# Sixteen half-height transposes instead of eight full ones, in four units of a retention and SiLU kernel

## The chip, the cores and the metric

The kernel runs on one core of one Trainium2 chip. Its time is the device time of one execution in microseconds (us). TensorE (PE) multiplies matrices and writes to PSUM, a memory of eight banks of 128 partitions; VectorE (DVE) and ScalarE (ACT) do element-wise work and bring results from PSUM to SBUF; GpSimd (POOL) prepares data; SyncE (SP) issues most DMA transfers. Each engine works through its own list of instructions in order and waits on semaphores of the others.

## The reference

A retention recurrence over 768 positions, for 4 batches and 8 heads of 64, followed by a feed-forward block with a SiLU:

```
for t in range(S):                       # S = 768
    state = gamma * state + outer(k[:, :, t], v[:, :, t])
    y[:, :, t] = (1 / sqrt(D)) * q[:, :, t] @ state        # D = 64
x = y as (3072, 512)                     # 4 * 768 tokens, 8 heads * 64
h = x @ w_in                             # w_in 512 x 2048
out = (h * sigmoid(h)) @ w_out           # w_out 2048 x 512
```

`gamma` has one value for each head. Results are float32.

## The kernel before

The recurrence is computed in chunks of 128 positions. A **unit** is one chunk of one batch, so there are 6 x 4 = 24 units, numbered chunk by chunk: unit n is chunk n // 4 of batch n % 4. For each unit the kernel does the following:

- *Transposes* (`stage_t`, L441): k and q arrive as 128 positions (partitions) by 8 heads by 64. Four transposes each on TensorE, one per pair of heads, against a 128x128 identity, put them into one PSUM bank each, `kp` and `qp`; ScalarE copies each bank as a whole into SBUF, `kt` and `qt` (L450). These are 128 partitions (two heads by 64) by 4 pairs by 128 positions.
- *Scores and sums* (`stage_s` L464, `stage_a` L474): within a unit the 128 positions are two halves of 64. Products of k and q inside a half, and of k and v for the running state, are 64x64 matmuls on quarters of the array, into the bank pair `sc`. `stage_s` reads k after it was multiplied by decay factors (`scale_k`, L390), which is done in place once the transposes have read it. For units 10 to 13 ScalarE does it, one head at a time (L399), four heads directly and four from the list `behind_copy`.
- *Masking and state* on VectorE (`steps_a`: `am` L482, `mid` L490, `state` L494), and scaling of `qt` (`scale_q`, L411).
- *Output of the unit* (`stage_y`, L513): more 64x64 matmuls into the bank pair `y`, in two parts. A small POOL instruction (`fence`, L385) stands between them.
- *Splitting* (`split_x`, L569 to L575) into three parts, which are the input `xt` of the feed-forward block.

From unit 14 on (`FAR`) k and q are turned by DMA instead, and no transposes run on TensorE.

The feed-forward block works on groups (c, f), chunk c and 128 of the 2048 hidden columns. A group is 12 matmuls of 128x512 (`multiply`, L666) into two banks, `ha` and `hb`. ScalarE copies `ha` (L676), VectorE subtracts `hb` (L681), ScalarE applies the SiLU (L686), and SP stores the group (`gd<-g`, L692). The banks `ha`, `hb` and `kp` take turns on three PSUM banks (`turn`, L376); `qp` has a bank of its own. The results wait in three buffers with the tag `hs` until their stores have landed.

Weights arrive as 64-bit numbers and are converted on the way: one ScalarE instruction (`ca`, L202), six on VectorE (L205 to L223), and then a split into three parts on both engines (`wi`: L120, L123, L126, L128). A group cannot run before its slice is there.

TensorE's order is that of the program text. The other engines' lists are written out by hand up to the first group of chunk 1 (L894 to L899). After that a planner orders them, with `queue(instruction)` holding a piece of work behind a named instruction; `evac[0]`, the last copy of the transposes, is one of these. Units 10 to 13 come just behind that point: the visits of units 10, 11 and 12 lie in two halves between the groups listed in `pairs` (L905), and unit 13 follows the last of them in one piece.

Of the kernel before, what the change touches and what calls it, by code (L numbers as in the profile page):

```python
# [13 lines left out]
FP32 = mybir.dt.float32  # L14
# [19 lines left out]
def kernel(  # L34
# [28 lines left out]
    nc = tc.nc  # L63
    B, H, S, D = q.shape
    DM, DF = moe_w_in.shape
    C = 128
    NC = S // C
    HP = H // 2
# [12 lines left out]
    def pool(name, bufs, **kw):  # L81
        return ctx.enter_context(tc.tile_pool(name=name, bufs=bufs, **kw))
# [6 lines left out]
    one = pool("one", 1)  # L89
# [49 lines left out]
    kqv = {"k": {}, "q": {}, "v": {}}  # L139
    EARLY = 2 * B  # L140

    FAR = 3 * B + 2
    LATER = 4 * B + 2
    early = {}

    def load(name, n):
        if n >= len(units):
            return
        c, b = units[n]
        src = {"k": k, "q": q, "v": v}[name]  # L150
        if n == 4 * B and name == "k":
            t = conv.tile([128, H, D], FP32, tag="wl", name=f"kf_{n}")
            nc.sync.dma_start(out=t, in_=src[b, :, ds(c * C, C)].rearrange("h t d -> t h d"))
            kqv[name][n] = t
            return
        if n < EARLY:

            if n not in early:
                early[n] = wpool.tile([128, 3, H, D], FP32, tag=f"w{4 + n}", name=f"kqv_{n}")
            t = early[n][:, "kqv".index(name)]  # L160
        else:
            t = ld.tile([128, H, D], FP32, tag=f"{name}f", name=f"{name}f_{n}",
                        bufs=2 if name == "q" else 3)
        nc.sync.dma_start(out=t, in_=src[b, :, ds(c * C, C)].rearrange("h t d -> t h d"))
        kqv[name][n] = t
# [86 lines left out]
    evac, held, w_sb = [], [], {}  # L252
    written = [True]

    def queue(ins):

        return ExitStack() if written[0] or ins is None else tc.issue_after(ins)
# [58 lines left out]
    ident = const.tile([128, 128], FP32, tag="ident", name="ident")  # L316
# [45 lines left out]
    xt, kt, qt, am = {}, {}, {}, {}  # L362
# [8 lines left out]
    def banks(tag, name, n=2):  # L371
        return ps_u.tile([128, n, 512], FP32, tag=tag, name=name)
# [3 lines left out]
    def turn(name):  # L376
        turns[0] += 1
        return ps_h.tile([128, 512], FP32, tag=f"h{turns[0] % 3}", name=name)
# [11 lines left out]
    def scale_k(n):  # L390
        if 0 <= n < len(units):
            t = kqv["k"][n]
            if units[n][0] == NC - 1:
                t = t[:D]
            if 2 * B + 1 < n < 3 * B + 2:

                def half(heads):
                    for h in heads:
                        nc.scalar.activation(out=t[:, h, :], in_=t[:, h, :], func=AF.Copy,  # L399
                                             scale=gk[:, units[n][0], h : h + 1])  # L400

                half(range(H // 2))
                behind_copy.append(lambda: half(range(H // 2, H)))
                return
            g = gk[: t.shape[0], units[n][0], :].unsqueeze(2).to_broadcast([t.shape[0], H, D])
            nc.vector.tensor_tensor(out=t, in0=t, in1=g, op=ALU.mult)
# [33 lines left out]

    def stage_t(n):  # L441

        for name, to, bufs, src, tp in (
                ("kt", kt, 2, kqv["k"][n], turn(f"kp_{n}")),
                ("qt", qt, 3, kqv["q"].pop(n), banks("q", f"qp_{n}", 1)[:, 0])):
            tp = tp.rearrange("p (a t) -> p a t", a=HP)
            for a in range(HP):
                nc.tensor.transpose(tp[:, a, :], src[:, 2 * a : 2 * a + 2, :], ident)
            to[n] = one.tile([128, HP, C], FP32, tag=name, name=f"{name}_{n}", bufs=bufs)
            evac[:] = [nc.scalar.copy(out=to[n], in_=tp).ins]  # L450

    def score_tile(n):
        u = banks("s", f"sc_{n}")
# [156 lines left out]
    def halves(m):  # L610

        first, mid, last = (0 <= m - i < len(units) for i in range(3))
        if first and m < FAR:
            stage_t(m)
# [5 lines left out]
        if mid:  # L620
# [9 lines left out]
            if m > 3 * B + 1 and units[m - 1][1] == B - 1:  # L630

                behind_copy.append(next_chunk)
        if first and m < LATER - 1 and m != FAR:
            with queue(masked[0]) if m > FAR else ExitStack():
                scale_k(m)
# [3 lines left out]

        n = m if m >= LATER else m + 1  # L640
        if FAR < n < len(units) and (m < LATER - 1 or m >= LATER):
            with queue(fenced[0]):
                part_t(n)
        for name in "kqv":
            for n in (m + 1, m + 2):
                if (n, name) not in apart and EARLY <= n <= LATER and n == (
                        m + 1 if name == "v" or n >= LATER else m + 2):
                    load(name, n)
# [6 lines left out]

    apart = [(FAR + 1, "k"), (FAR + 1, "q"), (FAR + 2, "q")]
    pending, stored = [], []
# [88 lines left out]
    def T(n):  # L746
        stage_t(n)
# [185 lines left out]
    first_far = steps.index((2, 3))  # L933
    parts = {first_far: FAR}
    turns_at = {first_far + 2: FAR}
    turns_at.update({far[m] + 1: m + 1 for m in range(FAR, LATER - 1)})
    joins_at = {far[m] + 1: m for m in range(FAR, LATER)}
# [47 lines left out]
    for c in range(NC):  # L985
# [9 lines left out]
        for f in range(NF):  # L995
            n = c * NF + f
# [3 lines left out]
            t = ready[n]  # L1000
# [17 lines left out]
        for b in range(B):  # L1018
            oa, ob = acc[b]
            o = one.tile([128, DM], FP32, tag=("kt", "qt")[b % 2], name=f"o_{c}_{b}",  # L1020
                         bufs=(2, 3)[b % 2])
# [8 lines left out]
            n = 2 if b == B - 1 else 1  # L1030
# [36 lines left out]
```

## Time and profile before

| | us |
|---|---|
| median of 4 runs | 618.06 (617.33 to 620.19) |
| the profiled execution | 618.18 |
| its span | 616.2 |
| TensorE busy | 597.9 |
| VectorE busy | 425.2 |
| ScalarE busy | 315.8 |
| one transpose, k or q, as recorded (L448) | 0.27 |
| one copy of its bank (L450), kt and qt | 0.57 and 0.59 |

The granted TensorE clock was 0.999 over the span. The span runs from the first to the last instruction; the execution's time is 2.0 us longer. Engine names in the lines are PE, PEld (TensorE's weight loads), DVE, ACT, POOL and SP. `out<-in` names the tiles that an instruction writes and reads, without buffer numbers; `x4` counts instructions; a 64x64 float32 matmul has two records, a transpose has one. A bracket at the end of a line tells how long the engine sat idle before it, and what ended the wait. Matmuls overlap, so the recorded length of one is longer than the distance from its start to the start of the next.

The transposes of units 10 to 13 start at 57.27, 66.22, 75.17 and 84.13 us.

### The profile page before, as it was taken

Reading aid. Unit: us, or ns where it says so; the run is one execution under the profiler, and the core shown is the slowest. Engines: PE = TensorE matmul, PEld = TensorE weight load, DVE = VectorE, ACT = ScalarE, POOL = GpSimd, SP = SyncE. Lnnn points to the kernel's source line nnn. Section 1 sums busy time; section 2 is a strip of 40 time slices with the busy share of each in tenths; the row PEclk is TensorE's granted clock in tenths of the full one; section 3 lists DMA queues with packets and bytes.
Section 4 is the critical chain, followed back from the end, with each engine's and each line's share of the span. In section 5 each row is a group of like instructions: output and inputs, shape, how many; then the busy total and the mean of one; then the engine's idle time right before and its main releaser. Section 6 shows DMA issues by size and latency. Waiting matters only on the chain.

```text
span 616.2 us, 13460 instructions
## 1 busy us (share of the span) xinstructions
PE 597.9 (97%) x5360; PEld 491.7 (80%) x5360; DVE 425.2 (69%) x731; ACT 315.8 (51%) x595; POOL 29.5 (5%) x85
## 2 busy tenths in 40 slices
PE   5798999999999999999999999999999999999997
PEld 4677887888778888888788888888888888888886
DVE  4899989799988777786699774635545463644631
ACT  7678886676667567666588732312221321312311
POOL 3000000100031111220000000000000000000000
PEclk9999999999999999999999999999999999999999
DMA  9998865784789699999777542532423433432301
GB/s 193 224 234 213 236 193 171 196 245 162 261 216 211 188 270 246 275 231 313 256 250 246 197 129 68 173 101 103 170 71 136 137 105 101 148 125 94 112 1 68
DMA packets 144334, 108.88 MB, mean 177 GB/s; under 512 B 101136, under 2 KB 109584, under 8 KB 144272
## 3 DMA queue, kind: packets, MB, share of 16 engines
q1 hardware_dynamic: 141392, 102.79, 59.2%
q10 hardware_dynamic: 2880, 5.24, 2.3%
q8 instruction: 42, 0.69, 0.5%
q14 instruction: 20, 0.16, 0.1%
HBM read 66.06 MB, written 36.70 MB: 167 GB/s over the span
## 4 chain that ended last, share of the span: by engine, by line
PE 76%; DVE 5%; ACT 1%; issue 1%; DMA 1%; DVEq 0%; POOLq 0%
PE o L1007 21%; PE ha L666 20%; PE oa L1007 14%; PE hb L666 10%; PE ob L1007 7%; PE y L513 2%; DVE g L681 1%; DMA yr<-yd 1%; PE sc L474 1%; PE sc L464 1%; DVE ca L218 1%; DVE xt L572 1%; PE o L1015 0%; DVE xt L575 0%; DVE cw L223 0%
## 5 line engine op out<-in xcount | busy, mean ns | idle before, releaser
L666 PE MATMUL ha<-xt,wi 128*128 128x512 f32 x768 | 193.8, 394 | 1.4 <-ACT xt L569 0.7
L666 PEld LDWEIGHTS ha<-xt,wi 128*128 128x128 f32 x768 | 141.8, 188 | 33.7 <-ACT wi L126 1.2
L1007 PE MATMUL o<-wo,gs 128*128 128x512 f32 x564 | 143.2, 389 | 0.0
L733 DVE TENSOR_TENSOR gs<-gr,gs 128x512 fp32r<-128x512 f32 x96 | 62.2, 685 | 90.3 <-ACT gs L731 90.3
L1007 PEld LDWEIGHTS o<-wo,gs 128*128 128x128 f32 x564 | 105.9, 188 | 21.9
L731 ACT ACTIVATE gs<-gr 128x512 fp32r<-128x512 f32 x96 | 53.6, 621 | 134.2 <-issue 131.8
L1007 PE MATMUL oa<-wo,gs 128*128 128x512 f32 x376 | 115.8, 389 | 0.0
L666 PE MATMUL hb<-xt,wi 128*128 128x512 f32 x384 | 102.9, 390 | 0.3 <-DVE xt L575 0.2
L681 DVE TENSOR_TENSOR g<-g,hb 128x512 f32<-128x512 f32 x96 | 65.5, 683 | 34.7 <-ACT g L676 21.8
L666 PEld LDWEIGHTS hb<-xt,wi 128*128 128x128 f32 x384 | 71.9, 188 | 16.1 <-DVE xt L575 0.7
L686 ACT ACTIVATE g<-g 128x512 f32<-128x512 f32 x96 | 60.2, 628 | 45.4 <-DVE g L681 45.4
L1007 PEld LDWEIGHTS oa<-wo,gs 128*128 128x128 f32 x376 | 70.6, 188 | 14.7
L1007 PE MATMUL ob<-wo,gs 128*128 128x512 f32 x188 | 73.7, 392 | 0.0
L676 ACT ACTIVATE g<-ha 128x512 f32<-128x512 f32 x96 | 57.0, 593 | 27.9 <-PE ha L666 14.6
L734 DVE SCALAR_TENSOR_TENSOR gs<-gs 128x512 fp32r<-128x512 f32 x96 | 62.0, 683 | 0.0
L1007 PEld LDWEIGHTS ob<-wo,gs 128*128 128x128 f32 x188 | 35.3, 188 | 8.7 <-DVE o L1025 1.6
L202 ACT ACTIVATE ca<-wf 128x512 f32<-128x512 f32 x32 | 21.4, 668 | 7.3 <-DVE cw L223 5.0
L1024 ACT ACTIVATE o<-o 128x512 f32<-128x512 f32 x10 | 6.0, 600 | 33.4 <-PE o L1007 33.0
L218 DVE SCALAR_TENSOR_TENSOR ca<-wf,ca 128x512 f32<-128x512 uint32 x32 | 22.7, 710 | 0.5
L482 DVE TENSOR_TENSOR am<-sc,decay 128x512 f32<-128x512 f32 x24 | 16.5, 687 | 9.5 <-PE sc L474 9.4
L212 DVE SCALAR_TENSOR_TENSOR cs<-ca,cs 128x512 uint32<-128x512 uint32 x32 | 22.1, 690 | 0.9
L513 PE MATMUL y<-qt,mid 64*64 64x64 f32 x384 | 19.7, 220 | 1.8 <-POOL token L385 1.8
(93 smaller groups left out, 563.2 us busy)
## 6 DMA issues: line engine op xcount, KB each, us to landing
gd<-g SPq DMA_DIRECT2D x96, 256.0 KB, 3.5
gr<-gd SPq DMA_DIRECT2D x96, 256.0 KB, 2.7
wf<-in_moe_w_out_dram SPq DMA_DIRECT2D x16, 512.0 KB, 5.0
out_dram<-o ACTq DMA_DIRECT2D x20, 256.0 KB, 2.1
wf<-in_moe_w_in_dram SPq DMA_DIRECT2D x16, 256.0 KB, 4.2
wf<-in_moe_w_in_dram SPq DMA_DIRECT2D x32, 128.0 KB, 3.9
kf<-in_k_dram SPq DMA_DIRECT2D x16, 256.0 KB, 4.2
qf<-in_q_dram SPq DMA_DIRECT2D x16, 256.0 KB, 4.2
```

Source lines behind the costliest of these rows:

```text
L202: nc.scalar.activation(out=a.bitcast(FP32), in_=hi.bitcast(FP32), func=AF.Abs, scale=65536.0)
L212: nc.vector.scalar_tensor_tensor(out=s, in0=a, scalar=3, in1=s, op0=ALU.logical_shift_left, op1=ALU.bitwise_or)
L218: nc.vector.scalar_tensor_tensor(out=p.bitcast(FP32), in0=lo, scalar=2.0 ** -52, in1=p.bitcast(FP32), op0=ALU.mult, op1=ALU.mult)
L513: i = nc.tensor.matmul(yp[ts(e, D), o, a, :], lhsT=lhsT, rhs=rhs, start=(e, o) not in started, stop=True, skip_group_check=True).ins
L666: nc.tensor.matmul(hb if i == 2 else ha, lhsT=w_sb[f][:, i, ts(kk, 128)], rhs=xt[c][:, i, kk, :], start=kk == 0 and i != 1, stop=kk == KIN ...
L676: copied[:] = [nc.scalar.activation(out=hs, in_=ha, func=AF.Copy, scale=ONE_E).ins]
L681: taken_out[:] = [nc.vector.tensor_tensor(out=hs, in0=hs, in1=hb, op=ALU.subtract).ins]
L686: nc.scalar.activation(out=hs, in_=hs, func=AF.Silu)
L731: nc.scalar.activation(out=t[:, 0, :], in_=g, func=AF.Copy, scale=HALF)
L733: nc.vector.tensor_tensor(out=t[:, 1, :], in0=g, in1=high, op=ALU.subtract)
L734: nc.vector.scalar_tensor_tensor(out=t[:, 2, :], in0=t[:, 1, :].bitcast(FP32), scalar=-1.0 / EPS, in1=high, op0=ALU.mult, op1=ALU.add)
L1007: nc.tensor.matmul(o, lhsT=g, rhs=wo[f][:, i, :], start=f == 0 and i != 1, stop=f == NF - 1 and i != 0)
```

## The change

For units 10 to 13 (`ROWS`), each transpose of 128 positions becomes two of 64 positions: one reads partitions 0 to 63 with the upper left 64x64 of the identity, the other partitions 64 to 127 with the lower right. They alternate, so that neighbours use different halves of the array's rows. The bank `kp` now holds the first 64 positions of both k and q, the bank `qp` the last 64. Each bank is brought out by two copies of 128x256, one into half the positions of `kt`, one of `qt`; that makes four copies a unit instead of two. `evac` holds the last of the four. All other units stay as they were.

```diff
     FAR = 3 * B + 2
+    ROWS = range(2 * B + 2, FAR)
...
     def stage_t(n):
 
-        for name, to, bufs, src, tp in (
-                ("kt", kt, 2, kqv["k"][n], turn(f"kp_{n}")),
-                ("qt", qt, 3, kqv["q"].pop(n), banks("q", f"qp_{n}", 1)[:, 0])):
-            tp = tp.rearrange("p (a t) -> p a t", a=HP)
+        src = kqv["k"][n], kqv["q"].pop(n)
+        tp = turn(f"kp_{n}"), banks("q", f"qp_{n}", 1)[:, 0]
+
+        def new(name, to, bufs):
+            to[n] = one.tile([128, HP, C], FP32, tag=name, name=f"{name}_{n}", bufs=bufs)
+            return to[n]
+
+        made = ("kt", kt, 2), ("qt", qt, 3)
+        if n not in ROWS:
+            for i in range(2):
+                t = tp[i].rearrange("p (a t) -> p a t", a=HP)
+                for a in range(HP):
+                    nc.tensor.transpose(t[:, a, :], src[i][:, 2 * a : 2 * a + 2, :], ident)
+                evac[:] = [nc.scalar.copy(out=new(*made[i]), in_=t).ins]
+            return
+        tp = [t.rearrange("p (i a t) -> p i a t", i=2, a=HP) for t in tp]
+        for i in range(2):
             for a in range(HP):
-                nc.tensor.transpose(tp[:, a, :], src[:, 2 * a : 2 * a + 2, :], ident)
-            to[n] = one.tile([128, HP, C], FP32, tag=name, name=f"{name}_{n}", bufs=bufs)
-            evac[:] = [nc.scalar.copy(out=to[n], in_=tp).ins]
+                for o in range(2):
+                    nc.tensor.transpose(tp[o][:, i, a, :], src[i][ts(o, D), 2 * a : 2 * a + 2, :],
+                                        ident[ts(o, D), ts(o, D)])
+        made = [new(*m) for m in made]
+        for o in range(2):
+            for i in range(2):
+                evac[:] = [nc.scalar.copy(out=made[i][:, :, ts(o, D)], in_=tp[o][:, i]).ins]
```

## The prediction

> **What bounds the kernel now.** I read four views: the page's busy line, busy times by stretch around units 10 to 13, the order of time on TensorE there, and that on ScalarE. The page first:
>
> ```profile
> PE 597.9 (97%) x5360; PEld 491.7 (80%) x5360; DVE 425.2 (69%) x731; ACT 315.8 (51%) x595; POOL 29.5 (5%) x85
> ```
>
> TensorE is the bound over the whole. The change lies in 57 to 87 us, and there the shares look different (columns: stretch, length, then busy time of PE, PEld, DVE, ACT, POOL):
>
> ```profile
> 57.27:66.22 8.95, 8.95 (x161) 7.33 (x160) 7.47 (x15) 7.49 (x17) 0.09 (x1) 1.00 0.90 221
> 66.22:75.17 8.95, 8.95 (x161) 7.33 (x160) 8.54 (x17) 8.04 (x20) 0.09 (x1) 1.00 0.81 219
> 75.17:84.13 8.96, 8.96 (x162) 7.33 (x160) 8.38 (x15) 7.41 (x20) 0.09 (x1) 1.00 0.89 243
> ```
>
> TensorE never stops, but VectorE is busy 83 to 95%, ScalarE 83 to 90% and the DMA engines 81 to 90%: three others stand close behind. Next, TensorE in order of time (start, length, line, operation):
>
> ```profile
> 57.27 0.60 PE L448 MATMUL kp<-ident,kf 128*128 128x128 f32 x4
> 57.70 0.60 PE L448 MATMUL qp<-ident,qf 128*128 128x128 f32 x4
> 58.23 0.69 PE L513 MATMUL y<-am,vf 64*64 64x64 f32 x32
> ...
> 61.04 1.07 PE L666 MATMUL hb<-xt,wi 128*128 128x512 f32 x4
> 62.04 0.69 PE L464 MATMUL sc<-vf,kf 64*64 64x64 f32 x32
> 62.55 0.65 PE L474 MATMUL sc<-qt,kt 64*64 64x64 f32 x32
> 63.02 0.22 PE L513 MATMUL y<-qt,mid 64*64 64x64 f32 x2
> ```
>
> A unit's eight transposes cost 58.23 - 57.27 = 0.96 us; four units, 3.8 us of 616. That caps any gain. Last, ScalarE:
>
> ```profile
> 58.01 0.57 ACT L450 COPY kt<-kp 128x512 f32<-128x512 f32 x1
> 58.48 0.64 ACT L686 ACTIVATE g<-g 128x512 f32<-128x512 f32 x1
> 59.01 0.58 ACT L450 COPY qt<-qp 128x512 f32<-128x512 f32 x1
> ...
> 61.24 0.60 ACT L676 ACTIVATE g<-ha 128x512 f32<-128x512 f32 x1 [0.69 <-PE ha L666]
> 61.73 0.66 ACT L202 ACTIVATE ca<-wf 128x512 f32<-128x512 f32 x1
> 62.92 0.63 ACT L686 ACTIVATE g<-g 128x512 f32<-128x512 f32 x1 [0.53 <-DVE g L681]
> ```
>
> and what it does later, with the one place where TensorE then waits:
>
> ```profile
> 79.73 0.60 ACT L676 ACTIVATE g<-ha 128x512 f32<-128x512 f32 x1 [0.76 <-DMA gd<-g]
> ...
> 84.81 0.81 ACT L399 ACTIVATE kf<-kf,gk 128x64 f32<-128x64 f32 x3
> ...
> 96.25 0.61 ACT L126 ACTIVATE wi<-wil 128x512 fp32r<-128x512 f32 x1
> ```
>
> ```profile
> 96.92 0.50 PE L666 MATMUL ha<-xt,wi 128*128 128x512 f32 x1 [0.40 <-ACT wi L126]
> ```
>
> From 81.09 to 93.1 ScalarE has no idle time at all, and at 96.92 TensorE stands until ScalarE has finished a weight slice. Four matmuls of that group start from 95.41, 0.23 apart, so the fifth was due at 96.35 and the stop is 0.57 us. What TensorE saves before 96 comes through only if that slice comes sooner too.
>
> **The change, part by part.**
>
> *Transposes on TensorE.* Removed: 0.96 a unit. Added: sixteen of 64 positions. The nearest rows are the 64x64 matmuls: 32 records in 0.47 us (62.55 to 63.02), four at a time on four quarters of the array, eight rounds of 0.059. Sixteen pieces, two at a time on two halves of the rows, are eight rounds too: 0.47. Entering a 64-row form costs more than staying: hb to L464 takes 1.00 (61.04 to 62.04), hb to kp 0.92 (56.35 to 57.27), so 0.08; the first round after an entry costs another 0.05 (L464's 32 records take 0.51); leaving for the next form costs 0.10 (0.53 for the q transposes to y, 0.43 for the k ones). Sum 0.70: 0.26 saved a unit, 1.04 for four. Bounds: 0.36 saved, if no leaving is paid between the 64-row forms; 0.21 lost, if the halves don't overlap (16 x 0.059 + 0.23 = 1.17). I take 0.26, since the 64x64 matmuls already send both row halves into two banks.
>
> A weight load could spoil this:
>
> ```profile
> 47.75 0.20 PEld L448 LDWEIGHTS kp<-ident,kf 128*128 128x128 f32 x2
> ```
>
> One such load is 0.14 long (139 ns, the median of kp's) and the first two together 0.20, so the second starts 0.06 after the first: a 128-column load holds its path for about 0.06, no longer than a round. The Trainium skill's page "TensorE: Matmul & The Clock Gate", section "LDWEIGHTS (loading the stationary operand)", speaks against the change: a load takes its columns over 1.2 in ns, however few rows it has. By that rule, as an estimate, each half-height load still takes 107 ns, eight rounds 0.85, a unit 1.08: 0.12 lost instead of 0.26 saved. I go by the row.
>
> *Copies on ScalarE.* Two of 512 elements become four of 256. The old ones take 0.47 from start to start (58.01 to 58.48, 59.01 to 59.47), 0.10 under their 0.57. The 256-element copy mid<-sc (L488) lasts 0.373, so 0.27: 4 x 0.27 - 2 x 0.47 = +0.14 a unit. Bounds: 0 (exact halves), +0.55 (no overlap). In units 10 to 12 idle time covers it (0.69, 0.17 and 0.76 before the next ha copies); in unit 13 nothing does. As results they are early: kt and qt of unit 10 are first needed at 71.50, bank kp is next written at 63.36 (unit 13: 89.97, with its copies done by 87.8), bank qp at 66.66. These cost nothing.
>
> *Order on ScalarE.* The built instruction lists differ on two engines only, TensorE and ScalarE; SP's, POOL's and VectorE's stand as before, so no DMA is moved past another. On ScalarE one swap matters, in unit 10: the copy of ha (L676 at 61.24) now stands behind ca<-wf (L202). That one needs its buffer from VectorE's L223 (60.88, 0.69 long), so it starts at 61.60; the copy follows 0.57 later (57.44 to 58.01), at 62.17 instead of 61.24, and ends at 62.77. Queued behind it: VectorE's L681 (62.20, now 62.80), the silu (62.92, now 63.50), the copies ys and xt, and the slice's L120 (64.67, now 65.2). VectorE's L123 (65.47) needs that result: 65.2 + 0.62, so 65.85, 0.4 late. From there to 71.8 VectorE has no idle time; L223 (70.59) ends 0.4 late, ScalarE's ca at 71.32 waits for exactly that, and the silu, ys and SP's stores go with it. The copy at 79.73 waits for the landing of the store issued at 73.61: 0.4 late. Bounds: 0 (the DMA, or the 0.34 that VectorE idles at 72.22, takes it up) to 0.6 (the whole of L681's delay). I take 0.4: the wait at 72.22 is on TensorE, which now comes 0.5 earlier.
>
> *Where the saving goes.* TensorE reaches the sc matmuls of unit 12 (85.84) 1.04 early, at 84.80. They need k scaled by L399, three pieces from 84.81 to 85.62, now until 86.0. So a new wait of about a microsecond, TensorE on ScalarE, takes the place of the saving. Unit 13's copies add 0.14; L126 goes from 96.25 to 96.8, the matmul from 96.92 to 97.45. Behind 97 all is paced by TensorE and moves along.
>
> Sum: -1.04 on TensorE, not passed on; +0.4 +0.14 on the chain through ScalarE, about +0.5. The profiled execution took 618.18 (span 616.2 and 2.0 around), 0.12 over the median 618.06: 618.18 + 0.5 - 0.12 = 618.6.
>
> **Rivals.**
>
> *The saving passes (1.04 less, 617.0).* The slice would have to come early as well: the store of 73.61 took 6.0 us to land where the median is 3.6, and L223 would have to be on time. For it: idle time of 0.3 to 0.7 on VectorE and ScalarE in each unit. Against: no idle time from 81.09 to 93.1.
>
> *The halves don't overlap.* TensorE comes 4 x 0.21 = 0.85 late to 96.35, into a stop of 0.57 that lengthens anyway: +0.5 to +0.85, 618.9. For it: no row shows a 64-row, 128-column tile. Against: the 59 ns rounds.
>
> *Each change of half empties the array (slower).* Place: between any two of the sixteen. Price: 0.059 + 0.09 apiece, 16 x 0.15 + 0.23 = 2.6 a unit, 1.65 lost, 6.6 for four, less the 0.57 of the stop: +6.0, 624. It decides once pieces stand more than 83 ns apart ((1.85 + 0.57)/4 = 0.6 over 0.96, less 0.23, over 16). Against: quarters follow each other in 15 ns.
>
> *The lag on ScalarE and VectorE feeds itself* through late stores, whose three buffers the next copies need: 0.4 in each of five pairs of groups, +2.0, 620.6.
>
> **How the numbers follow.** 0.3% is about what a measurement here can tell from no change: 1.85 us, 616.2 to 619.9. Forecast 0.50 (by its bounds +0.1 to +1.0: 618.1 to 619.0); saving passes 0.19; no overlap 0.13; these three are all within 0.3%: 0.82. Array emptied 0.08 and lag that feeds itself 0.06: slower 0.14. Faster 0.04: even 1.04 saved and the 0.57 stop gone make only 1.6, so it takes something not seen here. The range leaves the last three out (0.18): 616.9 to 619.9.
>
> **What would show it.** From kp to y 0.70 a unit instead of 0.96, pairs 0.06 apart. A wait of sc on ACT kf (L399's) near 85. The ca before g<-ha near 61.6 and that copy near 62.2. ha near 97.4 behind ACT wi. Transposes 0.1 or more apart, or ha before 96.5, would prove me wrong.

## The result and the profile after

The changed kernel takes 620.58 us (median of 53 executions, 618.41 to 628.33), the kernel before, run beside it, 619.01 (77 executions, 616.87 to 625.0). The ratio is 1.0029, with a 95% interval of 1.0018 to 1.0040: some 1.8 us slower (1.1 to 2.5), where 0.5 was forecast, and just inside the 0.3% that were set as the limit of what can be told. As a time it lies outside the range of 616.9 to 619.9. Half of the 2.0 us between it and the forecast is the base: the kernel before had a median of 618.06 in the four runs that the forecast started from and 619.01 here. Executions of one kernel differ by their granted clock (of the kernel before, run beside e1 below, the median is 618.6 at a mean clock of 0.999 or more and 623.1 below 0.996), but this doesn't explain the difference: e1, the changed kernel again, is slower by 2.0 and 2.2 us in the same two groups.

The profiled execution took 624.17 (span 622.4), well above the median, so it shows where time is lost, and its amounts hold for itself alone. To compare two profiles I take the start of each of TensorE's matmul groups, count it from the first group of unit 10 (54.23 us before, 55.58 after), and subtract. The 5.99 us between the two profiled executions are then:

| stretch (time in the profile before) | longer after, us |
|---|---|
| start to unit 10 | +1.35 |
| units 10 to 13, up to 87 us | -0.45 |
| 87 to 102 us | +0.56 |
| 102 to 198 us | +0.09 |
| 198 to 310 us | +4.42 |
| 310 us to the end | +0.01 |

The first row is not the change's: the code before unit 10 is the same. Most of it is the clock. In the profile before, records of the 64x64 products are some 26 ns apart up to 7.8 us and 14.6 ns from there; in this one they keep to 26 until 15.3 us, and 0.9 us of delay is left of that at 24 us. From 27.1 to 30.5 us the granted clock is 0.5 in this execution and 1.0 in the one before, which adds 1.0 us and shows as the 8 in the second slice (15.6 to 31.1 us) of the page's clock row. Ahead of unit 10 0.6 us of the 1.9 are made up, since TensorE idles 0.87 us at 52.17 before and 0.28 at the same place after.

```profile
PEclk9899999999999999999999999999999999999999
```

Kernels with and without the change had the early or the late start of the full clock (below, e9 with it was early, e16 without it late).

The second row is the change as it was meant. TensorE in order of time in unit 10, after (start, length, line, operation, tiles, shapes):

```profile
58.16 0.62 PE L684 MATMUL hb<-xt,wi 128*128 128x512 f32 x2
58.71 0.27 PE L463 MATMUL kp<-ident,kf 64*128 64x64 f32 x1
58.71 0.27 PE L463 MATMUL qp<-ident,kf 64*128 64x64 f32 x1
58.82 0.22 PE L463 MATMUL kp<-ident,kf 64*128 64x64 f32 x1
58.82 0.22 PE L463 MATMUL qp<-ident,kf 64*128 64x64 f32 x1
...
59.20 0.22 PE L463 MATMUL qp<-ident,qf 64*128 64x64 f32 x1
59.35 0.69 PE L531 MATMUL y<-am,vf 64*64 64x64 f32 x32
```

The two halves of a pair start within 0.01 us of each other, pairs 0.06 apart. A unit now takes this long (stretch, length, busy PE, PEld, DVE, ACT, POOL, then granted clock, DMA share and GB/s):

```profile
58.62:67.35 8.73, 8.73 (x169) 6.98 (x168) 6.89 (x14) 7.02 (x18) 0.09 (x1) 1.00 0.93 223
```

That is 8.73 instead of 8.95 or 8.96, so 0.22 to 0.23 us saved a unit. TensorE reaches the sc matmuls of unit 12 0.93 us early; 0.48 of it is lost there, which leaves the 0.45 of the table. The third row takes back the rest: TensorE waits for a weight slice, as it did before, and starts at the same distance from unit 10 as before (98.39 - 55.58 = 42.81; before 96.92 - 54.23 = 42.69):

```profile
98.39 1.19 PE L684 MATMUL ha<-xt,wi 128*128 128x512 f32 x4 [0.41 <-ACT wi L126]
```

The fifth row, 198 to 310 us, is what nobody touched. Busy times of the stretch, before and after (stretch, length, busy PE, PEld, DVE, ACT, POOL, granted clock, DMA share, GB/s):

```profile
198.00:310.00 112.00, 111.63 (x1312) 91.98 (x1311) 84.94 (x148) 71.97 (x115) 14.01 (x20) 1.00 0.91 251
199.00:316.00 117.00, 113.12 (x1316) 92.13 (x1315) 84.80 (x149) 70.98 (x115) 14.09 (x20) 1.00 0.88 241
```

Its waits, before (engine and line <- what it waited for: us in total, times, longest):

```profile
DVE g L681 <- ACT g L676: 17.8, 16, 2.6
ACT g L676 <- DMA gd<-g: 4.0, 4, 1.4
```

and after:

```profile
DVE g L699 <- ACT g L694: 26.5, 14, 4.1
ACT g L694 <- DMA gd<-g: 11.7, 8, 2.8
PEld hb L684 <- ACT g L694: 5.3, 4, 1.8
ACT ca L203 <- DMA wf<-in_moe_w_out_dram: 5.2, 1, 5.2
PE hb L684 <- ACT g L694: 3.6, 4, 1.4
```

Read from below: TensorE's second group of a pair, hb, stands for ScalarE's copy of ha into a buffer of g (L694; L676 before), a wait of which the kernel before has a single case of 0.5 us. ScalarE's copy stands for the store of g (gd<-g), whose landing frees one of three buffers: 11.7 us instead of 4.0. The stores land late in a stretch where, in the profile before, the DMA engines are busy 0.91 of the time and TensorE 111.63 of 112 us.

### The profile page after: what moved, and what is told of

Same layout as the page of the kernel before. It is cut to its first block, busy times and chain, and to the rows that moved or that the text cites. A ratio compares the mean times of both kernels' runs of the same rounds, so it can differ in the third digit from the quotient of the medians.

```text
span 622.4 us, 13533 instructions
## 1 busy us (share of the span) xinstructions
PE 603.3 (97%) x5392; PEld 494.5 (79%) x5392; DVE 424.3 (68%) x731; ACT 315.1 (51%) x603; POOL 29.7 (5%) x85
## 4 chain that ended last, share of the span: by engine, by line
PE 75%; DVE 4%; DMA 3%; ACT 1%; issue 1%; DVEq 0%; SPq 0%; POOLq 0%; ACTq 0%
PE o L1025 21%; PE ha L684 19%; PE oa L1025 14%; PE hb L684 10%; PE ob L1025 7%; PE y L531 2%; DMA wf<-in_moe_w_out_dram 1%; DMA wod<-cw 1%; DMA yr<-yd 1%; PE sc L492 1%; DVE g L699 1%; PE sc L482 1%; ACT g L694 0%; PE o L1033 0%; DVE ca L219 0%
## 5 line engine op out<-in xcount | busy, mean ns | idle before, releaser
L694 ACT ACTIVATE g<-ha 128x512 f32<-128x512 f32 x96 | 56.8, 592 | 30.4 <-DMA gd<-g 14.4
```

The source lines that it names most:

```text
L694: copied[:] = [nc.scalar.activation(out=hs, in_=ha, func=AF.Copy, scale=ONE_E).ins]
```

## The experiments

Why should stores 100 us behind the change land later? Three theories. A: the new copies and the swapped order on ScalarE leave a lag behind that grows. B: TensorE comes out of unit 13 in another position against the transfers, and nothing but that matters. C came out of the first four runs.

### The change again, its order mended, its copies alone, its pieces one half after the other

e2 puts unit 10's ScalarE order back:

```
-        with queue(evac[0] if evac else None):
+        with queue(copied[0] if i == 4 else evac[0] if evac else None):
```

e3 keeps the eight full transposes of before and halves the copies only:

```
+            for o in range(2):
+                evac[:] = [nc.scalar.copy(out=to[:, :, ts(o, D)], in_=t[:, :, ts(o, D)]).ins]
```

e4 sends all lower halves first, then all upper halves, so that neighbours use the same half of the rows:

```
-        for i in range(2):
-            for a in range(HP):
-                for o in range(2):
+        for o in range(2):
+            for i in range(2):
+                for a in range(HP):
```

e1 is the changed kernel unchanged.

> The changed kernel as it is, beside the others on one chip, with a second profile. Theory A (the forecast's: ScalarE's swap in unit 10 and the added copies delay the weight slice that TensorE waits for at 97 us): about 1.003 of before, and the loss is there at 97 us, counted from unit 10's start. Theory B (the loss arises later, where ScalarE's copies of ha wait for stores of g to land, 200 to 300 us): also 1.003, but at 97 us the profile stands level with before, and 1 to 4 us are lost between 200 and 310 us again.

> Only ScalarE's order in unit 10 is mended: the copy of ha stands ahead of ca again, as before the change; everything else of the change stays. Theory A: the 0.4 us of the chain is gone, the ratio falls from 1.003 to about 1.000 (0.998 if the saving passes). Theory B: the swap is not the cause; 1.002 to 1.003 stays.

> The eight transposes of before, but four copies of 128x256 instead of two of 128x512, and no other difference in any engine's order. Theory A: +0.14 us in unit 13, hardly to be measured, 1.000 to 1.001. Theory B, with the copies as what shifts ScalarE: 1.002 to 1.003. If TensorE's earlier arrival is what shifts things: 1.000.

> All sixteen pieces as in the change, but the eight of the lower half first and then the eight of the upper half, so that neighbours use the same half of the rows. Theory A: pieces 0.06 apart, a unit about 1.2 us instead of 0.65, TensorE 0.85 us later at 84 us, ratio 1.003 to 1.004. Theory B: the ratio follows the stores and not TensorE's own time: 1.001 to 1.004, with no more loss than the 0.5 us of the pieces added.

Measured, ratio to the kernel before of the same session (619.87): e1 1.0046 [1.0024, 1.0069], e2 1.0055 [1.0029, 1.0081], e3 1.0005 [0.9978, 1.0032], e4 1.0036 [1.0008, 1.0065].

At 102 us the profiles differ as A says: e2 stands at -0.52 where after is at +0.11, so the swapped order costs 0.6 us there; the copies alone (e3) cost 0.53; pieces in turn cost 0.11 us for the first unit instead of saving 0.23. But by 310 us e1 has lost 2.07 more, e2 2.46, e4 2.05 and e3 0.53. A falls as the cause of the total: the mended order is no faster, and three kernels with different lags lose about the same. What the losers share, and e3 does not, is the sixteen pieces.

Then the transfers themselves. One store of g, issued 158.3 to 159.4 us on the time line of before, lands in 1.99 us before and 2.01 in e3, but in 2.89, 3.38, 3.42 and 3.10 in after, e1, e2 and e4. Its row before and after (KB, us to landing):

```profile
gd<-g SPq DMA_DIRECT2D x1, 256.0 KB, 2.0
gd<-g SPq DMA_DIRECT2D x1, 256.0 KB, 2.9
```

The DMA queues around it, before (window 158 to 162 us; queue, packets, MB, share):

```profile
q1 hardware_dynamic: 357, 0.86, 60.3%
q14 instruction: 1, 0.01, 0.5%
```

and after (the same window counted from unit 10, 159.35 to 163.35):

```profile
q1 hardware_dynamic: 289, 0.59, 46.8%
q8 instruction: 1, 0.02, 1.5%
q14 instruction: 1, 0.01, 0.5%
```

Queue 8 brings TensorE's instructions (a reading that the idle times further down bear out), in 42 packets of 16 KB over the span, each 0.9 to 2.3 us long. Its row on the page before:

```profile
q8 instruction: 42, 0.69, 0.5%
```

In before and e3 this packet comes at 165.7 and 165.1, in the four others at 159.3 to 159.5. The sixteen pieces are eight matmuls more a unit, 32 records and 32 loads in all: 64 instructions, a quarter of a packet if one holds 256. (The Trainium skill, "Runtime: NRT & Kernel Launch", section "Instruction fetch mechanics", gives blocks of 16 KiB, 256 instructions, fetched by the sequencer's own DMA queue. The trace agrees: 42 packets for 5360 records and as many loads.) A block of this stage lasts 28 us (137.7 to 165.7), so a quarter is 7 us, and 6 was found. Hence theory C: the pieces move the moments at which TensorE's instruction blocks are fetched, and at the new moments they meet stores that have no slack.

### Instructions added where TensorE is idle

If C holds, 64 TensorE instructions anywhere ahead must do the harm without any change to units 10 to 13, and a number that makes a whole block must undo it. e5, e8 and e6 are the kernel before with 16, 32 and 64 products of a zeroed tile (four instructions each: two records, two loads) ahead of the first unit; e7 is the kernel after with 48, which with the pieces make 256.

```
+    pad = const.tile([D, D], FP32, tag="pad", name="pad")
+    nc.vector.memset(pad, 0.0)
...
+        if n == 0:
+            idle = ps_h.tile([128, 512], FP32, tag="h0", name="idle")
+            for _ in range(16):
+                nc.tensor.matmul(idle[:D, :D], lhsT=pad, rhs=pad, start=True, stop=True)
```

> The kernel before with 16 products of a zeroed 64 by 64 tile put on TensorE ahead of the first unit, where it waits for its first operands (idle until 4.09 us in the profile before). They are 32 matmul records and 32 loads, as many TensorE instructions as the sixteen pieces add in units 10 to 13; units 10 to 13 themselves stay as before. Theory C (the position of the instruction blocks): TensorE's instructions come in blocks of 16 KB through a DMA queue of their own, 42 in the span; 64 instructions more put every later block a quarter of a block earlier, and where a block falls on a store of the feed-forward part the store lands about 0.9 us later (in the four profiles with pieces the block that was at 165.7 us comes at 159.4 and the store issued at 158.9 us lands in 2.9 to 3.4 us instead of 2.0). C expects the loss of the change without the change: 1.3 to 3 us slower than before, ratio 1.002 to 1.005, blocks at 130 and 159 to 161 us, and TensorE late by 1 to 4 us between 198 and 310 us. Theory A (the pieces or the copies of units 10 to 13 themselves) and theory B (TensorE's earlier phase after unit 12 meets the stores of g) expect the time before, ratio 0.998 to 1.001 (an earlier full clock at the start could take off up to 0.5 us).

> The same with 64 products, 256 instructions: one whole block of 16 KB, so that the later blocks fall where they fell before. Any cost of the padding itself is here four times as large as with 16. Theory C expects the time before, ratio 0.998 to 1.002, and the blocks at their old places (137 and 165 us). A theory by which the padding costs by its own time expects the start later by up to 1 us and at least four times what 16 products lose. A and B: the time before.

> The kernel after, with 48 such products ahead of the first unit: 192 instructions, which with the 64 of the pieces make one whole block, so that the blocks after unit 13 fall where they fell in the kernel before. Theory C expects the loss to go: ratio 0.997 to 1.001 to the kernel before (the 0.1 to 0.7 us that the pieces save may show), blocks at 137 and 165 us, and no loss of more than 1 us between 198 and 310 us. Theories A and B, by which the pieces, the copies or the earlier phase do it, expect the time after: ratio 1.002 to 1.005 and the waits of the groups for ScalarE's copies of g between 198 and 310 us.

> The kernel before with 32 such products, 128 instructions, half a block. A and B expect the time before. C expects some place of the blocks between the two others, blocks near 123 and 152 us; which stores they meet there can't be read from the traces at hand: between 1 us faster and 3 us slower, and the difference to 16 and 64 products, whatever its sign, comes between 150 and 310 us, not at the start.

e5 1.0039 [1.001, 1.0067], e8 1.009 [1.0059, 1.012], e6 1.0144 [1.0118, 1.017], e7 1.0069 [1.0041, 1.0096]. In the kernel before the totals grow with the number of products (e5, e8, e6), which is what C was not to show, and e7 missed the 0.997 to 1.001 that C expected; the profiles say why. The 32 records of 16 products took 3.67 us at the start, 0.11 each: every one went to the same quarter of the array, and the full clock had not come yet (at a granted clock of 1.0 such records took 0.06 in e9, below). So unit 10 starts at 55.7, 56.7, 65.3 and 62.0 us. From unit 10 on it is as C says: 6.33 us lost between 198 and 310 us in e5, none in e6 and e7; e8, half a block off, loses 3.6 us ahead of 198, 1.4 of it at a granted clock of 0.5 (201 to 204 us of its profile).

### The same with a cheaper place

So the products were put in front of the third and fourth units' y, where TensorE waits for masked scores: 48 under the change (e9), 48 under the change with the order mended (e11), 16 and 64 in the kernel before (e10, e12). In e10:

```
+            for _ in range({3: 16}.get(n, 0)):
+                nc.tensor.matmul(yp[:D, 0, 0, :], lhsT=pad, rhs=pad, start=True, stop=True,
+                                 skip_group_check=True)
```

> The kernel after, with 48 products of a zeroed tile (192 instructions) that cost next to nothing where they stand: ahead of the third and fourth units' y, where TensorE waits 0.7 and 0.9 us for the masked scores in the profile before (20 and 28 products, 0.6 and 0.8 us at the 14.6 ns a record of the scores). Ahead of the first unit they had delayed the start by 2 to 11 us, which is in the way of the totals. Theory C (the position of TensorE's instruction blocks): with the 64 instructions of the pieces they make a whole block, the loss goes, and the 0.1 us that the change keeps from units 10 to 13 is left: ratio to the kernel before 0.998 to 1.001, less than 1 us lost from unit 10 to the end. Theories A and B (the pieces, the copies, or TensorE's earlier phase): the time after, ratio 1.002 to 1.005, and 2 to 5 us lost between 198 and 310 us. Theory D (in the padded runs it was the late start that gave the transfers a lead, and no block): as A and B.

> The kernel before with 16 such products (64 instructions, as many as the pieces add) ahead of the fourth unit's y alone, in a wait of 0.9 us. C: the loss of the change with no piece in the kernel, ratio 1.001 to 1.006, and 1 to 6 us lost between 198 and 310 us with the TensorE block of 165.7 us at 159 to 161 us. A, B and D: the time before, ratio 0.999 to 1.001.

> The kernel after with unit 10's ScalarE order put back (which left TensorE 0.6 us earlier at 97 us than after does) and the 48 products. C: the 0.5 us at 97 us lasts to the end, ratio 0.997 to 1.000, the shortest of the four. A, B and D: 1.002 to 1.006 as without the products.

> The kernel before with 64 such products (256 instructions, one whole block), 28 and 36 of them ahead of the third and fourth units' y. C: the time before plus what of the 1.9 us of products doesn't fit into the two waits (0 to 0.5 us): ratio 0.999 to 1.002. A theory by which the products cost by their number: four times the loss of 16 products, 1.004 to 1.02. A, B and D: the time before, plus the same 0 to 0.5 us.

e9 1.0029 [1.0006, 1.0053], e10 1.0043 [1.0009, 1.0076], e11 1.0041 [1.0013, 1.0069], e12 1.0035 [1.0011, 1.0059]. From unit 10 to the end: e9 -0.07 (after: +4.63), e10 +5.17 with no piece in it, e11 -0.43, e12 +0.46. The waits between 198 and 310 us tell the two sorts apart. e10, the kernel before and 64 instructions:

```profile
ACT g L681 <- DMA gd<-g: 11.8, 9, 2.7
PEld hb L671 <- ACT g L681: 4.9, 5, 2.6
```

e9, the changed kernel and 192 instructions:

```profile
DVE g L704 <- ACT g L699: 15.4, 16, 2.6
ACT g L699 <- DMA gd<-g: 3.7, 3, 1.8
```

11.8 us as in after, 3.7 as before: the damage moved to the kernel without the change and left the one with it. The store issued near 159 us lands in 2.79 us in e10, in 2.03, 2.02 and 2.02 in e9, e11 and e12. A and B fall with this: e10 has neither the pieces nor the copies, and where TensorE stands at 102 us against before doesn't tell the two sorts apart, here or later (-0.52 to +0.31 us in the eight kernels that lose, -0.73 to +1.45 in those that don't). D, by which the late start and no block had spared the padded runs, falls with e13 and e17 below: their unit 10 starts at 55.90 and 55.53 us, and the first loses nothing, the second 5.9 us. But the totals of e9, e11 and e12 are still above before by 0.3 to 0.4%; their unit 10 starts at 60.6, 63.0 and 59.5 us, since 40 records in front of one y took 2.5 us (e9 and e11; 56 took 3.5 in e12) and the granted clock was 0.5 for 6.8 us of the start in e9 and 10.2 in e11.

### On four quarters of the array

e13 to e16 are after with 48, the mended order with 48, and before with 16 and with 64 products that take turns on the four quarters, as the scores do. In e13 and e14:

```
+            for k in range({2: 20, 3: 28}.get(n, 0)):
+                o, j = ts(k // 2 % 2, D), ts(k % 2, D)
+                nc.tensor.matmul(yp[o, k % 2, 0, :], lhsT=pad[j], rhs=pad[j], start=True,
+                                 stop=True, skip_group_check=True)
```

> The kernel after with 48 products of a zeroed tile (192 instructions, with the pieces' 64 one whole block) ahead of the third and fourth units' y, on the four quarters of the array in turn, 1.4 us if they run like the scores (29 ns each), nearly all of it in two waits. Theory C (blocks' position): less than 0.5 us lost from unit 10 to the end, ratio 0.998 to 1.002. If the position of the blocks shows only in single profiles and the change's +0.3% has another cause (A, B): 1.002 to 1.005.

> The same with unit 10's ScalarE order put back. C: 0.4 us gained from unit 10 to the end, ratio 0.997 to 1.001, below that of the run before in the same call by 0 to 0.7 us. A, B: 1.002 to 1.006.

> The kernel before with 16 such products (64 instructions, as many as the pieces add) ahead of the fourth unit's y: 0.5 us in a wait of 0.9 us. C: 1.3 to 5 us lost between 198 and 310 us, ratio 1.002 to 1.007, the spread of the single times wider than that of the whole-block kernels. A, B: the time before, 0.999 to 1.001.

> The kernel before with 64 such products, one whole block. C: nothing lost after unit 10, the start later by 0 to 1 us: ratio 0.999 to 1.002. A theory by which the products cost by their number: above e15's. A, B: the same as C here.

e13 1.0026 [1.0004, 1.0047], e14 1.0029 [1.0012, 1.0046], e15 1.0074 [1.0046, 1.0103], e16 1.0079 [1.006, 1.0099]. From unit 10 to the end: e13 +0.06, e14 -0.58, e15 +2.54, e16 -0.06, as C expects. The totals again did not follow: e13 and e14 were to come out at 1.002 and 1.001 at most, e16 level with before. Its start shows something else. TensorE in order of time, e16 (the bracket is the idle time ahead of the row; "issue" means that it waited for nothing the profile shows):

```profile
26.42 0.59 PE L476 MATMUL sc<-qt,kt 64*64 64x64 f32 x11 [2.40 <-issue]
```

and e15, where the idle time falls into the middle of one y, between the 9th and 10th of 32 equal records:

```profile
26.18 0.91 PE L515 MATMUL y<-am,kqv 64*64 64x64 f32 x23 [2.24 <-issue]
```

The kernel before has two such rows:

```profile
20.55 0.34 PE L513 MATMUL y<-am,kqv 64*64 64x64 f32 x6 [0.73 <-issue]
52.17 0.38 PE L474 MATMUL sc<-qt,kt 64*64 64x64 f32 x9 [0.87 <-issue]
```

Up to 75 us the twenty profiles have 46 such rows, and counted from the first matmul of the program every one stands within two of record 346, 473, 600, 727, 1107 or 1234: the spacing is 127 records, or a multiple of it; 127 records and as many loads make, with a few further instructions, 256. It is so whatever stands there: an am product in before, a zero product in e13, a score in e16. And all 46 idle times end 1.1 to 1.7 us after a packet of queue 8 has ended. So TensorE was waiting for its next instruction block, for 0.2 to 2.5 us. In the opening stage, where a product passes in 29 ns, blocks are used up as fast as they come, every 4 to 6 us in before, and the products that were to cost nothing came with a start up to 5 us later (e16, 59.19 against 54.23 us, some of it by the clock: the full clock came late, and from 26.0 to 29.4 us it was 0.5).

### Later in the program

e17 and e18, the kernel before, have the same products ahead of the eighth unit's y (16), and ahead of the fifth to eighth units' (16 each). e18's first line, the rest as above:

```
+            for k in range({4: 16, 5: 16, 6: 16, 7: 16}.get(n, 0)):
```

> The kernel before with 16 products of the zeroed tile (64 instructions) ahead of the eighth unit's y alone, some 0.5 us. Theory C (position of TensorE's instruction blocks): 0 to 1 us later at unit 10 and 1.3 to 5 us lost between 198 and 310 us; ratio 1.002 to 1.008. A, B (the pieces, the copies, the earlier phase): 0 to 1 us in all, ratio 1.000 to 1.0016.

> The same with 64 products (256 instructions, one whole block), 16 each ahead of the fifth to eighth units' y: 1.9 us of TensorE if nothing covers them. C: 0.5 to 3 us later at unit 10, nothing lost between 198 and 310 us; ratio 1.001 to 1.005, and the time below that of 16 products or level with it. By the number of the products alone it would be four times the loss of 16.

e17 1.0051 [1.0023, 1.0079], e18 1.0072 [1.0039, 1.0105]. e17 is the cleanest case of harm without the change: unit 10 at 55.53 us, level with after, 5.89 us lost between 198 and 310 us, a median 2.7 us over before's. e18 lost 0.01 us there, but its total missed what C expected: unit 10 started at 64.26 us, with a granted clock of 0.5 in three stretches of 3.4 us (from 29.4, 43.1 and 63.6 us) and idle times of 2.3, 2.1, 0.9 and 1.8 us for "issue" up to 62 us.

### All profiles side by side

The block is the TensorE instruction packet that comes at 165.7 us in before, counted from unit 10 like the rest.

| kernel | TensorE instructions added | block at, us | lost 198 to 310, us |
|---|---|---|---|
| before | 0 | 165.7 | 0 |
| e3, copies alone | 0 | 165.1 | 0.5 |
| after | 64 (pieces) | 159.4 | 4.4 |
| e1, after again | 64 (pieces) | 159.5 | 2.1 |
| e2, order mended | 64 (pieces) | 159.3 | 2.5 |
| e4, halves in turn | 64 (pieces) | 159.4 | 2.1 |
| e5, before | 64 | 160.0 | 6.3 |
| e10, before | 64 | 159.5 | 5.5 |
| e15, before | 64 | 159.2 | 2.5 |
| e17, before | 64 | 159.5 | 5.9 |
| e8, before | 128 | 151.1 | 0.2 (3.6 from 102 to 198) |
| e6, e12, e16, e18, before | 256 | 166.0 to 167.3 | 0.0 in each |
| e7, e9, e13, after | 64 (pieces) + 192 | 165.7 to 166.8 | 0.0 in each |
| e11, e14, order mended | 64 (pieces) + 192 | 164.9, 166.3 | 0.2, 0.0 |

Eight profiles with the block at 159 to 160 lose 2.1 to 6.3 us, eleven with it at 165 to 167 lose 0.5 at most, on both sides with and without the pieces. In e5 and e10 1.6 us of the loss fall into 3.4 us at a granted clock of 0.5 (from 273.2 and 276.2 us of their profiles); without these the eight lose 2.1 to 5.9. The store issued near 159 us lands in 2.8 to 3.5 us in all eight and in 2.0 in the eleven. That the position of the blocks decides this loss is shown. In size it is of the order of the totals (1.1 to 2.5 us for the change, 1.5 to 4.3 for e1), and 64 instructions put into the kernel before slow its total too (e5, e10, e15 and e17, 1.0039 to 1.0074); but single profiles lose from 2.1 to 6.3 us, so that it makes up the whole of the total is not shown.

Open stays: by how much a total gains when the blocks are put back. No run brought the total of the changed kernel back to that of before: e7, e9 and e13, with whole blocks, are at 1.0069, 1.0029 and 1.0026. The products have a cost at the start that can hide the gain, since the kernel before with 64 of them loses nothing after unit 10 either and still is at 1.0144, 1.0035, 1.0079 and 1.0072 (e6, e12, e16, e18). In e13 and e14 nothing is lost after unit 10 (+0.06 and -0.58 us), and still the medians are 1.2 and 1.6 us above before's; their profiled starts (55.90) are 0.2 to 0.3 us behind those of after and e1 and 1.7 behind that of before; how much of that is the products and how much the late clock of these two profiles can't be told for the medians. Open in part is the path from the late store at 159 us to the stretch behind 198. Three stores on the way are late as well: the one issued at 161.3 us takes 4.2 to 4.8 us in the losing profiles, against 3.4 to 3.9 in the others; the one at 179.1 takes 4.0 to 4.9 in all eight, against 2.5 to 3.0 in ten of the eleven; and the one at 202.5 takes 3.4 to 4.4 (4.4 in after), against 2.0 to 2.1 (the first and the last where the trace has their landing). What hands the delay from one to the next is not shown. And a version faster than both was not found: mended order with whole blocks (e14) keeps 0.58 us behind unit 10, too little for a total to show, and its start gives that away.

## Why the prediction was wrong

- **Transposes, 0.26 saved a unit.** Near: 0.22 to 0.23. The halves overlap in pairs, 0.06 apart. The load row (second load 0.06 behind the first) was the right guide; by the load rule of the Trainium skill's page "TensorE: Matmul & The Clock Gate", section "LDWEIGHTS (loading the stationary operand)", a unit would have lost 0.12.
- **Copies, +0.14 a unit.** Near: +0.10. New copies start 0.25 to 0.27 apart, so four take about 1.04 us instead of 0.94. ScalarE in order of time, after, unit 10:

```profile
60.38 0.38 ACT L468 COPY qt<-kp 128x256 f32<-128x256 f32 x1
60.63 0.40 ACT L468 COPY kt<-qp 128x256 f32<-128x256 f32 x1
60.90 0.41 ACT L468 COPY qt<-qp 128x256 f32<-128x256 f32 x1
...
62.95 0.70 ACT L203 ACTIVATE ca<-wf 128x512 f32<-128x512 f32 x1 [0.93 <-DVE cs L224]
63.54 0.59 ACT L694 ACTIVATE g<-ha 128x512 f32<-128x512 f32 x1
```

- **The swap in unit 10.** Right in place and size: less the 1.35 of the later start, ca stands at 61.60 and the copy at 62.19 (forecast 61.60 and 62.17). It cost 0.6 us at 102 us (e2 against after), where 0.4 was taken and 0.6 was the upper bound.
- **The saving isn't passed on.** Right in kind. The new wait near 85 was to cost about 1 us; TensorE came 0.93 early and lost 0.48 there, and another 0.56 up to the slice, whose matmul started 0.1 after before's time, counted from unit 10, where 0.5 was forecast.
- **"Behind 97 all is paced by TensorE and moves along."** This step failed. It holds to 198 us (+0.09) and then breaks: 4.4 us in the profile of after, 2.1 in its repetition. I had costed the pieces as time on the array, and as nothing anywhere else. They are also 64 more entries in TensorE's instruction stream, and the page showed that this stream comes by DMA (42 packets on queue 8). The sum lacked that term. What the runs showed in its place: with 64 instructions more, pieces or not, the block of 165.7 us comes at 159 to 160, the store issued near 159 us lands 0.8 to 1.5 us later, and 2.1 to 6.3 us are lost between 198 and 310 us.
- **The rival of 620.6, a lag that feeds itself through late stores whose three buffers the next copies need,** named the wait that appeared and by chance its size, but not the cause: with the order mended the loss stays, and with instructions added to the kernel before it comes without any lag. Its price was worked out from ScalarE's lag, 0.4 us in each of five pairs of groups, so that 620.6 is so near the measured 620.58 is luck.
- **"The halves don't overlap" and "each change of half empties the array"** fell to the rows above. In e4, where neighbours use the same half, a unit lost 0.1 us, less than the 0.21 priced for halves that don't overlap; e4 changes the half only once a unit, so it says nothing of the second.
- **Chances.** Change of nothing measurable had 0.82 and the ratio, 1.0029, is just within that limit, with half of its interval beyond it. The range was too narrow above, by the missing term, as far as it makes up the total, and by a base 0.95 us lower than in the later runs.

## What to carry to other kernels

An edit that changed the number of TensorE's instructions moved every later fetch of its instruction blocks, and in a stretch where the DMA engines and TensorE were both nearly full (0.91 and 0.997), that alone cost the profiles 2.1 to 6.3 us, more than the 1.04 that the edit was to gain. Before explaining a small loss far behind a change, look where the instruction packets fall in both profiles, and try the old kernel with as many idle instructions more, and the new one with as many as make a whole block; put them where they cost nothing themselves, or compare the profiles behind them, as had to be done here. And compare profiles from a mark just ahead of the change, since what lies before it can differ by more than the effect.

## What the runs showed of the hardware that was not expected

- TensorE can starve for instructions. In the opening stage of 64x64 products it stood idle for 0.2 to 2.5 us at the edges of blocks of 256 instructions, even between two records of one y (2.24 us in e15), until 1.1 to 1.7 us after a packet of queue 8 had ended. The Trainium skill's page "Runtime: NRT & Kernel Launch", section "Instruction fetch mechanics", calls the crossing of such an edge mostly hidden; here it was hidden in before and after from unit 10 on, where no such row of a matmul stands, and not in the opening.
- A fetch of 16 KB is felt by data. Over the twenty profiles there are 253 transfers for which a TensorE packet began within 2 us of their issue in some and not in others; with it they landed 0.54 us later in the mean, 69 stores of g among them 0.51 us.
- Where a zero product goes decides its price: 0.06 us a record at a granted clock of 1.0 when all went to one quarter of the array (e9, e12) and 0.11 at 0.5 (e10), but 0.015 on four quarters in turn, 16 products 0.69 us in all (e15).
- The full clock came at 7.8 us in some executions and at 15.3 in others of the same opening, worth 0.9 to 1.3 us at 24 us (e4, after and e1 against before; a stretch of 3.4 us at a granted clock of 0.5, from 27 us on, cost each of the three another 0.7 to 1.0): records of the first y are 0.69 us for 32 in before, e9 and e15, 1.13 in after, e12 and e16.
